# A retention layer with routed experts: dense 64-column state, half of the key decays on ScalarE, ranks from the one-hots, and routing put ahead of two weight splits

## The chip, the cores and the metric

One core of one Trainium2 chip runs the program. The metric is device microseconds (us) of one execution. TensorE is called PE here (PEld are its weight loads), VectorE DVE, ScalarE ACT, GpSimd POOL; SP issues most of the transfers (SPq is its queue).

## The reference

Three layers follow one another. With lam a decay per head (8 heads of 64, 2 batches of 768 tokens):

```python
# 1. retention, block by block (here blocks of 64; the kernel takes 128)
intra = (q_b @ k_b.T * Dmask) @ v_b
inter = (q_b * lam_pow) @ kv_state
out_b = intra + inter
kv_state = lam_block * kv_state + (k_b * rev_pow).T @ v_b
# 2. top-1 mixture of 8 experts (512 -> 1024 -> 512) over the 1536 tokens
logits = x @ w_gate + modality_bias[modality_id]
e = argmax(logits); gate = softmax(logits)[e]
y = gate * (relu(x @ w1[e]) @ w2[e])
# 3. dense layer (512 -> 2048 -> 512)
h = y @ w_in
out = (h * clip(h + 3, 0, 6) / 6) @ w_out
```

## The kernel before

Every engine but POOL runs its instructions in the order in which the program writes them, so a wait holds up whatever is written behind it on that engine. There are three stages.

**Retention** runs over 12 units `u`: 6 chunks `c` of 128 tokens, batch `b` 0 and 1 in turn. On PE a unit is: `scores(u+1)` (q against k, 64 rows by 64 rows, two PSUM banks), `rows(u-1)` (the finished unit turned to token rows and multiplied with the gate weights, tiles `xr`), `cross(u)` (q times state, `o_ps`, and decayed keys times v, `s_ps`), `inner(u)` (masked scores times v, also into `o_ps`). The state of two heads is a 128x128 block with zeros off the diagonal, so one full-array product serves both heads. POOL computes the decays (`k_d`, `q_d`, the decayed state `s_new`), DVE the masks `s_t`, the two `add`s of `s_ps` into `s_new`, and the routing; ACT copies `o_ps` to `x_t` and `xr` to `x_r` and multiplies `x_r` by the gate.

**Routing** is done once for each pair of units: `choose` (argmax as a one-hot `oh_all`), `rank` (how many earlier tokens chose the same expert: a triangle product plus a running count `acc_oh`), `place` (gate and place), `spot` (place as two one-hots, from which `sort_tokens` later writes the token lists to `order_d`).

**Experts** take slots of 264 tokens. The first, `LEAD`, is filled from the first four chunks while the last chunk is still being routed. A slot has eight pieces of weights: four of `w1` (`step` computes two hidden blocks `h_hi`, `h_lo` each) and four of `w2` (one output block each). `w_split(n)` cuts a weight into two parts: ACT writes the high one (`whi`), DVE, or POOL for pieces 0 and 1, the low one (`wlo`). `step` calls `w_split(n+2)` first. After each block `pump` writes a few instructions of the routing (`tail`, then `table`) into the queues; the table gives expert and tokens of the next slot, which SP reads to load weights and the token list `ix`, and POOL gathers the tokens `xg`. Then come dense blocks, in which nothing is touched.

Of the kernel before, what the change touches and what calls it, by code (L numbers as in the profile page):

```python
# [54 lines left out]
def retention_moe_ffn(ctx, tc, qT, kT, kn, vn, lam, mod, w_gate, bias, w1, w2, win, wout, out):  # L55
# [147 lines left out]
    def w_split(n, low=None):  # L203
        if n >= len(pieces):
            return
        raw = raws.pop(n)
        hi = wh.tile([P, 8, P], F32R, tag="whi", name="whi")
        lo = wh.tile([P, 8, P], F32R, tag="wlo", name="wlo")
        nc.scalar.copy(hi.rearrange("p a f -> p (a f)"), raw)  # L209
        (low or nc.vector).tensor_tensor(  # L210
            out=lo.rearrange("p a f -> p (a f)"), in0=raw,
            in1=hi.bitcast(F32).rearrange("p a f -> p (a f)"), op=ALU.subtract)
        ws[n] = (hi, lo)
# [29 lines left out]
    def step(n, fill=(), rate=4):  # L243
# [4 lines left out]
        if early:  # L248
            w_split(n + 2)
# [4 lines left out]
        if nxt is not None and s == LEAD and q == NP1 + 1:  # L254
            x_gather_next(nxt)
# [51 lines left out]
    with ExitStack() as ac:  # L307
# [66 lines left out]
        acc_oh = acon.tile([P, B, E], BF16, name="acc_oh")  # L374
        nc.gpsimd.iota(acc_oh, pattern=[[0, B], [NT // P, E]], base=0, channel_multiplier=0,
# [72 lines left out]
        def decays(u):  # L448
            b, c = units[u]
            q_t, k_t, k_n, v_n = data[u]  # L450
            if c < NC - 1:
                kdec[u] = a2.tile([P, H, D], F32, tag="k_d", name="k_d")
                nc.gpsimd.tensor_tensor(
                    out=kdec[u], in0=k_n, in1=dmask[:, :, C - 1:C].broadcast_to([P, H, D]), op=ALU.mult)
            if c > 0:
                qd[u] = a2.tile([P, NPAIR, C], F32, tag="q_d", name="q_d")
                nc.gpsimd.tensor_tensor(out=qd[u], in0=q_t, in1=qdec, op=ALU.mult)
            if c < NC - 1:
                snew[u] = a2.tile([P, NPAIR, P], F32, tag=f"st{b}", name="s_new")
                if c == 0:  # L460
                    nc.gpsimd.memset(snew[u], 0.0)
                else:
                    nc.gpsimd.tensor_tensor(
                        out=snew[u], in0=state[b], in1=qdec[:, :, C - 1:C].broadcast_to([P, NPAIR, P]), op=ALU.mult)

        def cross(u):
# [4 lines left out]
            else:  # L471
                o_ps = ps_1.tile([P, NPAIR, C], F32, tag="y0", name="o_ps")
            if c > 0:
                for p in range(NPAIR):
                    nc.tensor.matmul(o_ps[:, p, :], state[b][:, p, :], qd[u][:, p, :], start=(p == 0), stop=False)
            adds = []
            if c < NC - 1:
                s_ps = ps_1.tile([P, NPAIR, P], F32, tag="y1", name="s_ps")
                kd2 = kdec[u].rearrange("p (a t) d -> p a (t d)", t=2)
# [31 lines left out]
        def rows(u):  # L511
# [10 lines left out]
            lp = a2.tile([P, 2, E], F32, tag="lp", name="lp")  # L522
            x_r = a2.tile([P, KD, P], F32, tag="x_r", name="x_r", bufs=4)
# [7 lines left out]
        def choose(c, b0, b1, fill):  # L531

            fill = list(fill)
            n = b1 - b0
            bb = slice(b0, b1)

            def gap():
                if fill:
                    fill.pop(0)()
# [15 lines left out]
            gap()  # L555
            first = a2.tile([P, n], F32, tag="first", name="first")
            nc.vector.tensor_reduce(out=first, in_=cand, axis=AX.X, op=ALU.max)
            gap()
            nc.vector.tensor_tensor(out=oh_all[:, c, bb, :], in0=rev2, in1=e2(first), op=ALU.is_equal)
            while fill:  # L560
                gap()
# [4 lines left out]
        def rank(c, b0, b1, count=None):  # L566

            n = b1 - b0
            rk = ps_r.tile([P, n + 1, E], F32, tag="rk", name="rk")
            oh = oh_all[:, c, b0:b1, :]  # L570
            nc.tensor.matmul(rk[:, :n, :], tri_bf, oh, start=True, stop=False)
            nc.tensor.matmul(rk[:, :n, :], ones_bf, acc_oh[:, :n, :], start=False, stop=(n == 1))
            if n == 2:
                nc.tensor.matmul(rk[:, 1, :], ones_bf, oh[:, 0, :], start=False, stop=True)
            if count is not None:
                nc.tensor.matmul(rk[:, n, :], ones_bf, acc_oh[:, 0, :], start=True, stop=False)
                for j in range(n):
                    nc.tensor.matmul(rk[:, n, :], ones_bf, oh[:, j, :], start=False, stop=(j == n - 1))
# [4 lines left out]
        def scale(c, b):  # L583
            x_r = pair[c]["x"][b]
            nc.scalar.activation(x_r, x_r, ACTF.Copy, scale=pair[c]["gate", b])

        def store(c, b):
            i = c * B + b
            x_r = pair[c]["x"][b].rearrange("p k d -> p (k d)")
            nc.sync.dma_start(out=x_d[i * P:(i + 1) * P, :], in_=x_r)  # L590

        def place(c, b0, b1, late=False):
# [14 lines left out]
            if late:  # L607
                return
            add = oh[:, 0, :]
            if n == 2:  # L610
                add = a2.tile([P, E], BF16, tag="t2", name="t2")
                nc.vector.tensor_tensor(out=add, in0=oh[:, 0, :], in1=oh[:, 1, :], op=ALU.add)
            nc.vector.tensor_tensor(
                out=acc_oh, in0=acc_oh, in1=add.unsqueeze(1).broadcast_to([P, B, E]), op=ALU.add)
# [83 lines left out]
        decays(0)  # L698
        put_off = []
        for u in range(NU):  # L700
# [25 lines left out]
            o_ps, adds = cross(u)  # L726
            if done:
                choose(*done, adds)
            else:
                for a in adds:  # L730
                    a()
            if u == NU - 2:
                w_split(0, nc.gpsimd)
            inner(u, o_ps)
            if done:
# [14 lines left out]

        tail = [
            lambda: None,
            lambda: None,
            lambda: (rank(NC - 1, 0, B, n_e), place(NC - 1, 0, B, True), scale(NC - 1, 0), scale(NC - 1, 1)),
            lambda: spot(NC - 1),
        ]
        rows(NU - 1)
        choose(NC - 1, 0, B, [])
# [278 lines left out]
```

## Time and profile before

| | us |
|---|---|
| runs shown: median of 3 | 516.55 (515.56 to 517.21) |
| profiled execution, its own time | 521.23 |
| profiled execution, span from first to last instruction | 519.4 |
| PE busy in the span | 488.5 (94%) |
| DVE busy | 331.9 (64%) |
| ACT busy | 209.3 (40%) |
| POOL busy | 77.6 (15%) |

The shares are means over the three stages. Retention ends at about 81 us of the span, the lead slot at about 115 us, and the dense layer starts at about 244 us. A row of a timeline has start, duration, engine, line, operation, output <- inputs, shapes, count, and in brackets the idle time before it with what ended it.

### The profile page before, as it was taken

To read this page: it belongs to the slowest core of one execution; us is meant where nothing else is said; L and a number is where in the kernel's file an instruction comes from. 1 tells how busy PE (TensorE), PEld (TensorE's weight loads), DVE (VectorE), ACT (ScalarE), POOL (GpSimd) and SP (SyncE) were. 2 spreads that over 40 slices of the span, in tenths; PEclk is the share of its full clock that TensorE was granted. 3 is DMA by queue.
4 is the path that set the end of the run, shared out by engine and by line. 5 is a ranking of instruction groups with operands and counts; after the bars stand their busy time and mean duration, and the time that the engine had idled before them with its cause. 6 is when DMAs were issued, how large, how long until landed. Compare 5 with 4: busy or idle time off the path is not lost.

```text
span 519.4 us, 8309 instructions
## 1 busy us (share of the span) xinstructions
PE 488.5 (94%) x3136; PEld 429.7 (83%) x3136; DVE 331.9 (64%) x659; ACT 209.3 (40%) x365; POOL 77.6 (15%) x92
## 2 busy tenths in 40 slices
PE   5999888869999999996999999999999999999995
PEld 5888777859999999996888888888888888888885
DVE  4799998856769877771465463667646666523252
ACT  0233445425566655651354544433424343222230
POOL 4766351060020310000000000000000000003023
PEclk9899999988999999998899999999999999999998
DMA  4976364465686878541221220312202220002022
GB/s 142 370 241 204 120 202 149 167 205 163 215 273 203 257 209 263 201 133 25 99 84 43 80 82 3 114 47 81 79 3 84 76 85 1 1 1 81 1 81 81
DMA packets 25324, 64.25 MB, mean 124 GB/s; under 512 B 5954, under 2 KB 6053, under 8 KB 25277
## 3 DMA queue, kind: packets, MB, share of 16 engines
q1 hardware_dynamic: 22173, 57.25, 33.8%
q0 software_dynamic: 2416, 6.39, 3.9%
q8 instruction: 26, 0.43, 0.4%
q14 instruction: 21, 0.17, 0.1%
q10 hardware_dynamic: 688, 0.01, 0.1%
HBM read 57.29 MB, written 6.34 MB: 123 GB/s over the span
## 4 chain that ended last, share of the span: by engine, by line
PE 51%; POOL 0%; POOLq 0%; DVE 0%; issue 0%
PE ph L920 26%; PE po L939 25%; POOLq L1033 0%; POOL out_y L986 0%; POOL out_y L948 0%; DVE acc L946 0%; DVE row L973 0%
## 5 line engine op out<-in xcount | busy, mean ns | idle before, releaser
L925 DVE SCALAR_TENSOR_TENSOR g<-r,ph 128x512 f32<-128x512 f32 x48 | 33.0, 688 | 67.8 <-ACT r L923 67.8
L939 PE MATMUL po<-wo_hi,g_lo 128*128 128x512 f32 x188 | 74.1, 394 | 0.0
L939 PE MATMUL po<-wo_lo,g_hi 128*128 128x512 f32 x188 | 74.0, 394 | 0.0
L939 PE MATMUL po<-wo_hi,g_hi 128*128 128x512 f32 x188 | 73.1, 389 | 0.0
L210 DVE TENSOR_TENSOR wlo<-wraw,whi 128x1024 fp32r<-128x1024 f32 x46 | 56.2, 1222 | 18.1 <-ACT whi L209 18.0
L923 ACT ACTIVATE r<-ph,half 128x512 f32<-128x512 f32 x48 | 33.0, 688 | 81.0 <-PE ph L920 71.9
L920 PE MATMUL ph<-y_hi,wi_hi 128*128 128x512 f32 x192 | 53.3, 400 | 4.0 <-DVEq L881 4.0
L948 POOL DMA_INDIRECT out_y<-acc,row x11 | 10.7, 969 | 307.2 <-DVE acc L946 304.2
L929 DVE TENSOR_TENSOR g_lo<-g,g_hi 128x512 fp32r<-128x512 f32 x48 | 33.2, 693 | 33.0 <-ACT g_hi L927 33.0
L920 PE MATMUL ph<-y_lo,wi_hi 128*128 128x512 f32 x192 | 53.9, 403 | 0.0
L920 PE MATMUL ph<-y_hi,wi_lo 128*128 128x512 f32 x192 | 53.2, 399 | 0.0
L209 ACT CAST whi<-wraw 128x1024 fp32r<-128x1024 f32 x48 | 50.2, 1045 | 4.1 <-DMA wraw<-in_w 4.1
L920 PEld LDWEIGHTS ph<-y_hi,wi_hi 128*128 128x128 f32 x192 | 36.8, 192 | 12.3 <-ACTq L881 4.2
L927 ACT CAST g_hi<-g 128x512 fp32r<-128x512 f32 x48 | 29.8, 621 | 36.2 <-DVE g L925 36.2
L920 PEld LDWEIGHTS ph<-y_hi,wi_lo 128*128 128x128 f32 x192 | 36.9, 192 | 8.8
L920 PEld LDWEIGHTS ph<-y_lo,wi_hi 128*128 128x128 f32 x192 | 36.6, 191 | 8.9
L939 PEld LDWEIGHTS po<-wo_lo,g_hi 128*128 128x128 f32 x188 | 35.3, 188 | 8.6
L939 PEld LDWEIGHTS po<-wo_hi,g_hi 128*128 128x128 f32 x188 | 35.4, 188 | 8.4
L939 PEld LDWEIGHTS po<-wo_hi,g_lo 128*128 128x128 f32 x188 | 35.3, 188 | 7.4
L222 POOL DMA_INDIRECT xg<-x_d,ix x18 | 22.5, 1250 | 96.0 <-DMA ix<-order_d 65.9
L269 PE MATMUL ps<-x_hi,whi 128*128 128x264 f32 x192 | 32.2, 291 | 1.8 <-DVE h_lo L273 1.6
L269 PE MATMUL ps<-x_lo,whi 128*128 128x264 f32 x192 | 31.7, 288 | 0.0
(176 smaller groups left out, 820.4 us busy)
## 6 DMA issues: line engine op xcount, KB each, us to landing
wraw<-in_w SPq DMA_DIRECT2D x48, 512.0 KB, 3.5
raw<-in_win SPq DMA_DIRECT2D x16, 512.0 KB, 3.8
raw<-in_wout SPq DMA_DIRECT2D x16, 512.0 KB, 4.2
q_t<-in_qT SPq DMA_DIRECT2D x12, 256.0 KB, 3.5
k_t<-in_kT SPq DMA_DIRECT2D x12, 256.0 KB, 4.8
v_n<-in_vn SPq DMA_DIRECT2D x12, 256.0 KB, 4.2
x_d<-x_r SPq DMA_DIRECT2D x12, 256.0 KB, 2.0
k_n<-in_kn SPq DMA_DIRECT2D x10, 256.0 KB, 7.8
```

Source lines behind the costliest of these rows:

```text
L209: nc.scalar.copy(hi.rearrange("p a f -> p (a f)"), raw)
L210: (low or nc.vector).tensor_tensor(out=lo.rearrange("p a f -> p (a f)"), in0=raw, in1=hi.bitcast(F32).rearrange("p a f -> p (a f)"), op=AL ...
L222: ld = nc.gpsimd.indirect_dma_start(out=xg, out_offset=None, in_=x_d[0:EARLY * B * P, :] if s == LEAD else x_d[:], in_offset=bass.Indirect ...
L269: nc.tensor.matmul(ps, w[:, 4 * f2 + k, :], x[:, k, :], start=(m == 0), stop=(m == 3 * KD - 1))
L920: nc.tensor.matmul(ph, w[:, f, k, :], y[:, k, cols], start=(n == 0), stop=(n == 3 * KD - 1))
L923: nc.scalar.activation(r6, ph, ACTF.Relu, scale=1.0 / 6.0, bias=half)
L925: nc.vector.scalar_tensor_tensor(out=g, in0=r6, scalar=1.0, in1=ph, op0=ALU.min, op1=ALU.mult)
L927: nc.scalar.copy(g_hi, g)
L929: nc.vector.tensor_tensor(out=g_lo, in0=g, in1=g_hi.bitcast(F32), op=ALU.subtract)
L939: nc.tensor.matmul(pos_[t], g[:, ts], w[:, f, :], start=(f == 0 and n == 0), stop=(f == FB - 1 and n == 2))
L948: rows_apart(nc.gpsimd.indirect_dma_start(out=out, out_offset=bass.IndirectOffsetOnAxis(ap=row[:, i:i + 1], axis=0), in_=acc[:, i, :], in_ ...
```

## The change

- `s_new` has 64 columns for each pair instead of 128: no zero halves, no memset. `cross` computes each head by itself: `o_ps` from 64 rows to 64 columns (rows and columns of one half each), `s_ps` from 128 rows to 64 columns with 64 moving columns. The two `add`s become one, which runs ahead of `choose` instead of between its instructions.
- Of `k_d`, heads 0 to 3 are written by four ACT instructions (`key_decays(u+1)`, behind `inner(u)`), heads 4 to 7 by POOL. `q_d` is written in two POOL instructions, the POOL weight splits in four.
- `rows` copies all of `xr` with ACT and DVE sums the logits from the copy, instead of two sums from PSUM ahead of the copies.
- `rank` adds up the one-hots of all earlier chunks on PE, `acc_oh` is gone; gated rows go to a tile of their own, `x_s`.
- In steps 0 and 1 `w_split(n+2)` comes after the blocks; `rank` and `place` of the last pair are put behind the first step's second block (before: the second step's first), `spot` behind the second step's first. The next slot's gather is put one step earlier.

```diff
@@ w_split
+        parts = 4 if low else 1
+        for j in range(parts):
+            js = slice(j * 8 // parts, (j + 1) * 8 // parts)
+            (low or nc.vector).tensor_tensor(
+                out=lo[:, js, :], in0=raw.rearrange("p (a f) -> p a f", f=P)[:, js, :],
+                in1=hi.bitcast(F32)[:, js, :], op=ALU.subtract)
@@ step
-        if early:
+        if early and n > 1:
             w_split(n + 2)
...
-        if nxt is not None and s == LEAD and q == NP1 + 1:
+        if nxt is not None and s == LEAD and q == NP1:
             x_gather_next(nxt)
...
                 pump(fill, rate)
+            if n < 2:
+                w_split(n + 2)
@@ decays
-                    out=kdec[u], in0=k_n, in1=dmask[:, :, C - 1:C].broadcast_to([P, H, D]), op=ALU.mult)
+                    out=kdec[u][:, KA:, :], in0=k_n[:, KA:, :],
+                    in1=dmask[:, KA:, C - 1:C].broadcast_to([P, H - KA, D]), op=ALU.mult)
...
+        def key_decays(u):
+            if units[u][1] < NC - 1:
+                k_n = data[u][2]
+                for h in range(KA):
+                    nc.scalar.activation(kdec[u][:, h, :], k_n[:, h, :], ACTF.Copy, scale=dmask[:, h, C - 1:C])
@@ cross
                 for p in range(NPAIR):
-                    nc.tensor.matmul(o_ps[:, p, :], state[b][:, p, :], qd[u][:, p, :], start=(p == 0), stop=False)
+                    for r in halves:
+                        nc.tensor.matmul(
+                            o_ps[r, p, :], state[b][r, p, :], qd[u][r, p, :], start=(p == 0), stop=False)
...
-                    nc.tensor.matmul(s_ps[:, p, :], kd2[:, p, :], v_n[:, p * P:(p + 1) * P], start=True, stop=True)
+                    for t, r in enumerate(halves):
+                        h = 2 * p + t
+                        nc.tensor.matmul(
+                            s_ps[r, p, :], kdec[u][:, h, :], v_n[:, h * D:(h + 1) * D], start=True, stop=True)
@@ rows
             for j in range(2):
-                nc.vector.tensor_reduce(
-                    out=lp[:, j, :], in_=xr[j][:, :, P:].rearrange("p k e -> p e k"), axis=AX.X, op=ALU.add)
-                nc.scalar.copy(x_r[:, 2 * j:2 * j + 2, :], xr[j][:, :, :P])
-            nc.vector.tensor_tensor(out=lg[:, b, :], in0=lp[:, 0, :], in1=lp[:, 1, :], op=ALU.add)
+                nc.scalar.copy(x_r[:, 2 * j:2 * j + 2, :], xr[j])
+            nc.vector.tensor_reduce(
+                out=lg[:, b, :], in_=x_r[:, :, P:].rearrange("p k e -> p e k"), axis=AX.X, op=ALU.add)
@@ rank
+            nc.tensor.matmul(rk, ones_bf, base_oh[:, :m, :], start=True, stop=False)
+            for a in earlier:
+                nc.tensor.matmul(rk, ones_bf, over(a, m), start=False, stop=False)
+            nc.tensor.matmul(rk[:, 1:, :], ones_bf, over(oh[:, 0, :], m - 1), start=False, stop=False)
...
+            nc.tensor.matmul(rk[:, :n, :], tri_bf, oh, start=False, stop=True)
```

How the queues change, at three places. First PE, from the ranks of chunk 1 to the end of the next unit (`rk` rank, `xr` rows, `o_ps` cross and inner, `s_ps` new state). Before:

```order
L571 LDWEIGHTS tri_bf
L571 MATMUL rk<-oh_all,tri_bf 128x16
L572 LDWEIGHTS ones_bf
L572 MATMUL rk<-acc_oh,ones_bf 128x16
L574 LDWEIGHTS ones_bf
L574 MATMUL rk<-oh_all,ones_bf 128x8
L521 MATMUL xr<-iw,x_t 128x136 x4
L475 MATMUL o_ps<-q_d,s_new 128x128 x4
L481 MATMUL s_ps<-v_n,k_d 128x128 x4
L501 MATMUL o_ps<-s_t,v_n 64x128 x8
```

And of the change, from behind the rank's first product:

```order
L583 LDWEIGHTS ones_bf
L583 MATMUL rk<-oh_all,ones_bf 128x16
L583 LDWEIGHTS ones_bf
L583 MATMUL rk<-oh_all,ones_bf 128x16
L584 LDWEIGHTS ones_bf
L584 MATMUL rk<-oh_all,ones_bf 128x8
L587 LDWEIGHTS tri_bf
L587 MATMUL rk<-oh_all,tri_bf 128x16
L539 MATMUL xr<-iw,x_t 128x136 x4
L491 MATMUL o_ps<-q_d,s_new 64x128 x8
L499 MATMUL s_ps<-v_n,k_d 64x64 x8
L519 MATMUL o_ps<-s_t,v_n 64x128 x8
```

The state's two groups have eight half-size products each instead of four, and the rank two products more for each earlier chunk.

Second ACT, from one unit's `x_t` to the next unit's `x_t`, with what each instruction waits for. Before:

```order
L505 COPY x_t<-o_ps 128x512 [waits PE_49,Activation_49]
L585 ACTIVATE x_r<-x_r,gate 128x512 [waits DVE_49,Activation_49]
L585 ACTIVATE x_r<-x_r,gate 128x512 [waits Activation_49]
L527 COPY x_r<-xr 128x256 [waits DMAHW2_49,DVE_49]
L527 COPY x_r<-xr 128x256 [waits DVE_49]
L505 COPY x_t<-o_ps 128x512 [waits PE_49]
```

And of the change:

```order
L523 COPY x_t<-o_ps 128x512 [waits PE_49,Activation_49]
L478 ACTIVATE k_d<-k_n,dmask 128x64 [waits DMAHW4_49,Activation_49,Pool_49]
L478 ACTIVATE k_d<-k_n,dmask 128x64 x3
L596 ACTIVATE x_s<-x_r,gate 128x512 [waits DMAHW2_49,DVE_49,Activation_49]
L596 ACTIVATE x_s<-x_r,gate 128x512 [waits DMAHW3_49,Activation_49]
L542 COPY x_r<-xr 128x272 [waits PE_49] x2
L523 COPY x_t<-o_ps 128x512 [waits PE_49]
```

The copies `x_r`, which stand ahead of `x_t`, waited for DVE and now wait for PE; four decays stand in between.

Third DVE, at the start of the lead slot, from the end of the last `choose` (`sm`) on; `wlo` is the low part of a weight, `n_e` to `gate` are the last pair's rank and place. Before:

```order
L563 TENSOR_REDUCE sm<-ex 128x2
L210 TENSOR_TENSOR wlo<-wraw,whi 128x1024
L273 SCALAR_TENSOR_TENSOR h_lo<-ps,h_hi 128x264 x2
L210 TENSOR_TENSOR wlo<-wraw,whi 128x1024
L273 SCALAR_TENSOR_TENSOR h_lo<-ps,h_hi 128x264
L580 TENSOR_TENSOR n_e<-rk,off_e 128x8
L596 TENSOR_TENSOR tmp<-rk,oh_all 128x16
L597 TENSOR_SCALAR sm<-sm 128x2
```

And of the change:

```order
L570 TENSOR_REDUCE sm<-ex 128x2
L277 SCALAR_TENSOR_TENSOR h_lo<-ps,h_hi 128x264 x2
L590 TENSOR_TENSOR n_e<-rk,off_e 128x8
L607 TENSOR_TENSOR tmp<-rk,oh_all 128x16
L608 TENSOR_SCALAR sm<-sm 128x2
L610 TENSOR_REDUCE dst_all<-tmp 128x2
L612 RECIPROCAL gate<-sm 128x2
L214 TENSOR_TENSOR wlo<-wraw,whi 128x1024
```

Two weight splits stood ahead of the last pair's rank; now they stand behind it.

## Rows read from the trace of the kernel before

**Rows 1.** Busy time by stretches: start:end, length, engines (instructions), PE clock granted, DMA share, GB/s.
```profile
39.00:52.00 13.00, 11.82 (x137) 10.80 (x134) 11.73 (x36) 4.04 (x10) 7.91 (x7) 1.00 0.62 204
...
91.00:104.00 13.00, 11.57 (x100) 11.22 (x99) 11.70 (x41) 6.48 (x12) 0.00 (x0) 1.00 0.49 167
104.00:117.00 13.00, 8.32 (x70) 7.78 (x70) 7.27 (x15) 3.79 (x7) 7.98 (x6) 0.87 0.68 204
```

**Rows 2.** Timeline of one pair of units: the wait, then PE's groups.
```profile
41.86 1.50 DVE L626 TENSOR_TENSOR at_b<-b_io,pos_b 128x256 f16<-128x256 int32 x1
...
44.42 0.24 DVE L525 TENSOR_REDUCE lp<-xr 128x8 f32<-128x16 f32 x2
...
45.15 0.60 ACT L505 COPY x_t<-o_ps 128x512 f32<-128x512 f32 x1
...
45.80 1.19 PE L521 MATMUL xr<-iw,x_t 128*128 128x136 f32 x8 [1.18 <-ACT x_t L505]
46.72 0.98 PEld L475 LDWEIGHTS o_ps<-q_d,s_new 128*128 128x128 f32 x8
...
47.62 0.97 PEld L481 LDWEIGHTS s_ps<-v_n,k_d 128*128 128x128 f32 x8
...
48.71 0.85 PEld L501 LDWEIGHTS o_ps<-s_t,v_n 128*64 128x64 f32 x16
...
49.74 0.97 PEld L443 LDWEIGHTS sc<-q_t,k_t 64*128 64x128 f32 x16 [0.17 <-issue]
```

**Rows 3.** Waits by pair, 13 to 81 us: total us, times, longest.
```profile
PE xr L521 <- ACT x_t L505: 4.0, 4, 1.2
...
PE rk L571 <- DVE oh_all L559: 2.3, 2, 1.7
...
PE xr L521 <- ACT x_r L527: 0.5, 1, 0.5
```

**Rows 4.** Groups by line and shape, 0 to 120 us: busy us, mean ns | idle before.
```profile
L457 POOL TENSOR_TENSOR q_d<-q_t,qdec 128x512 f32<-128x512 f32 x10 | 13.1, 1306 | 16.8 <-PE o_ps L475 10.3 <-issue 4.7 <-DMA q_t<-in_qT 1.4
...
L527 ACT COPY x_r<-xr 128x256 f32<-128x256 f32 x24 | 7.8, 377 | 23.6 <-DVE lp L525 23.6
...
L489 DVE TENSOR_TENSOR s_new<-s_new,s_ps 64x256 f32<-64x256 f32 x16 | 6.6, 415 | 0.2
...
L554 DVE SCALAR_TENSOR_TENSOR cand<-df,rev_e 128x16 f32<-128x16 f32 x6 | 5.3, 878 | 0.2
...
L552 ACT ACTIVATE ex<-df 128x16 f32<-128x16 f32 x6 | 1.3, 216 | 4.0 <-DVE df L550 4.0
```

**Rows 5.** Timeline, first and last of the three products of one rank.
```profile
50.83 0.18 PE L571 MATMUL rk<-oh_all,tri_bf 128*128 128x16 bf16 x1
...
50.90 0.17 PE L574 MATMUL rk<-oh_all,ones_bf 128*128 128x8 bf16 x1
```

**Rows 6.** Timeline of the start: ACT's table load, the first state product.
```profile
2.67 1.28 ACT L505 ACT_TABLE_LOAD   x1 [2.67 <-issue]
...
13.85 2.07 PE L481 MATMUL s_ps<-v_n,k_d 128*128 128x128 f32 x8
```

**Rows 7.** Timeline of the lead slot, 82 to 115 us.
```profile
82.08 2.40 POOL L210 TENSOR_TENSOR wlo<-wraw,whi 128x1024 fp32r<-128x1024 f32 x1 [4.16 <-ACT whi L209]
82.17 2.35 DVE L546 TENSOR_TENSOR lg<-lg,bias_tok 128x16 f32<-128x16 f32 x1
...
91.69 0.43 DVE L273 SCALAR_TENSOR_TENSOR h_lo<-ps,h_hi 128x264 fp32r<-128x264 f32 x1 [1.74 <-ACT h_hi L272]
...
99.87 0.17 DVE L817 SCALAR_TENSOR_TENSOR tab<-s_io,picks 128x13 int32<-128x13 f32 x1
...
100.44 0.40 PE L290 MATMUL py<-h_lo,whi 128*128 128x264 f32 x1 [1.13 <-DVE h_lo L273]
...
101.10 0.37 SPq L219 DMA_DIRECT2D ix<-order_d  x1
...
114.66 0.85 PE L236 MATMUL xt<-ident,xg 88*128 88x88 f32 x4 [2.14 <-DMA xg<-x_d,ix]
```

More of the change, by code (lines that the diff above doesn't have):

```diff
@@ L25 @@
 B, H, S, D = 2, 8, 768, 64
+KA = 4
 NPAIR = H // 2
@@ L373, in retention_moe_ffn @@
         nc.gpsimd.memset(zrow, 0.0)
-        acc_oh = acon.tile([P, B, E], BF16, name="acc_oh")
-        nc.gpsimd.iota(acc_oh, pattern=[[0, B], [NT // P, E]], base=0, channel_multiplier=0,
+        base_oh = acon.tile([P, B + 1, E], BF16, name="base_oh")
+        nc.gpsimd.iota(base_oh, pattern=[[0, B + 1], [NT // P, E]], base=0, channel_multiplier=0,
                        allow_small_or_imprecise_dtypes=True)
@@ L568, in rank @@
             n = b1 - b0
-            rk = ps_r.tile([P, n + 1, E], F32, tag="rk", name="rk")
+            m = n + (count is not None)
+            rk = ps_r.tile([P, m, E], F32, tag="rk", name="rk")
             oh = oh_all[:, c, b0:b1, :]
[L571 to L574, printed above, removed]
+            earlier = [oh_all[:, c2, b2, :] for c2 in range(c) for b2 in range(B)]
+            over = lambda a, k: a.unsqueeze(1).broadcast_to([P, k, E])
+            nc.tensor.matmul(rk, ones_bf, base_oh[:, :m, :], start=True, stop=False)
+            for a in earlier:
+                nc.tensor.matmul(rk, ones_bf, over(a, m), start=False, stop=False)
+            nc.tensor.matmul(rk[:, 1:, :], ones_bf, over(oh[:, 0, :], m - 1), start=False, stop=False)
             if count is not None:
-                nc.tensor.matmul(rk[:, n, :], ones_bf, acc_oh[:, 0, :], start=True, stop=False)
-                for j in range(n):
-                    nc.tensor.matmul(rk[:, n, :], ones_bf, oh[:, j, :], start=False, stop=(j == n - 1))
+                nc.tensor.matmul(rk[:, n, :], ones_bf, oh[:, 1, :], start=False, stop=False)
+            nc.tensor.matmul(rk[:, :n, :], tri_bf, oh, start=False, stop=True)
+            if count is not None:
                 nc.vector.tensor_tensor(out=count, in0=rk[:, n, :], in1=off_e, op=ALU.subtract)
@@ L584, in scale @@
             x_r = pair[c]["x"][b]
-            nc.scalar.activation(x_r, x_r, ACTF.Copy, scale=pair[c]["gate", b])
+            x_s = pair[c]["s", b] = a2.tile([P, KD, P], F32, tag="x_s", name="x_s")
+            nc.scalar.activation(x_s, x_r[:, :, :P], ACTF.Copy, scale=pair[c]["gate", b])
         def store(c, b):
             i = c * B + b
-            x_r = pair[c]["x"][b].rearrange("p k d -> p (k d)")
-            nc.sync.dma_start(out=x_d[i * P:(i + 1) * P, :], in_=x_r)
+            x_s = pair[c]["s", b].rearrange("p k d -> p (k d)")
+            nc.sync.dma_start(out=x_d[i * P:(i + 1) * P, :], in_=x_s)
         def place(c, b0, b1, late=False):
@@ L606, in place @@
                     store(c, b)
[L607 to L614, printed above, removed]
         def spot(c):
@@ L698, in retention_moe_ffn @@
         decays(0)
+        key_decays(0)
         put_off = []
@@ L726, in retention_moe_ffn @@
             o_ps, adds = cross(u)
+            for a in adds:
+                a()
             if done:
[L728 to L731, printed above, removed]
+                choose(*done)
             if u == NU - 2:
@@ L734, in retention_moe_ffn @@
             inner(u, o_ps)
+            if u + 1 < NU:
+                key_decays(u + 1)
             if done:
@@ L749, in retention_moe_ffn @@
                 lead_order()
+        rows(NU - 1)
+        choose(NC - 1, 0, B)
         tail = [
             lambda: None,
+            lambda: (rank(NC - 1, 0, B, n_e), place(NC - 1, 0, B, True)),
+            lambda: (spot(NC - 1), scale(NC - 1, 0), scale(NC - 1, 1)),
             lambda: None,
-            lambda: (rank(NC - 1, 0, B, n_e), place(NC - 1, 0, B, True), scale(NC - 1, 0), scale(NC - 1, 1)),
-            lambda: spot(NC - 1),
-        ]
-        rows(NU - 1)
-        choose(NC - 1, 0, B, [])
+        ]
         step(0, tail, 1)
```

41 lines of the change are left out of this document (14 added, 27 removed).

## The prediction

> **What bounds the kernel now.** I read the busy time by stretches first. From 39 to 52 us PE is busy 11.82 of 13 us and DVE 11.73, so neither covers for the other; in the lead slot (91 to 104) DVE has 11.70 and PE 11.57; from 104 to 117 PE has only 8.32 and its granted clock falls to 0.87, between the two levels [rows 1]. Behind that the dense layer keeps PE busy and nothing of it is changed, so what the change is worth is how much earlier PE gets through the first 117 us.
>
> Where PE waits in retention the waits by pair say: 4.0 us for `x_t` (four times), 2.3 us for a one-hot (twice), 0.5 us for `x_r` [rows 3]. The timeline shows the cause of the first: DVE's `at_b` takes 1.50 us, so the logit sums `lp` start only at 44.42; the `x_r` copies wait for them, `x_t` stands behind those in ACT's queue and starts at 45.15, and PE has waited 1.18 us when `xr` starts at 45.80 [rows 2]. It is late DVE work seen through ACT. In the lead slot a DVE addition of 16 elements runs from 82.17 to 84.52, as long as POOL's weight split, 82.08 to 84.48 [rows 7]. From there DVE is late to the end: PE waits 1.13 us for `h_lo` at 100.44, the table entry `tab` that names the next slot's tokens is started at 99.87, SP asks for the list at 101.10, and the last gathered tokens reach PE at 114.66 after 2.14 us of waiting [rows 7]. Those steps are a chain, so what is earlier at `tab` is earlier at 114.66.
>
> **The change part by part** (a minus is a gain).
>
> *ACT no longer waits for DVE.* `x_r` waits for PE alone, so the waits for `x_t` and `x_r` should go: -4.0 and -0.5 [rows 3]. ACT takes on four decays a unit. No row shows one; a 16-element activation takes 0.216 and a 256-element copy 0.377 [rows 4], so four cost 0.9 to 1.5 us. I take 1.0, as 64 elements lie near the small one. They stand behind `x_t` and are needed one scores, one rows and one cross group later: 1.03 (16 records, as in `inner`, 48.71 to 49.74) + 0.92 (45.80 to 46.72) + 0.90 (46.72 to 47.62) = 2.85 us [rows 2], so they are hidden; behind them wait the gate products and `x_r`, with ACT at 4.04 of 13 us [rows 1]. If that cover were gone, up to 1.5 us a unit would be on the path. At the start the table load (1.28 us, at 2.67 before, hidden) now stands with the first decay behind the keys' transfer; POOL's decay released the first state product at 13.85 [rows 6]. Bounds 0 and +1.3; I take 0, because PE then needs only half of the heads from ACT first and one at a time.
>
> *PE, cross.* Four full products take 0.90 us (46.72 to 47.62), 0.11 us for each of 8 records; the 16 records of `inner`, on two column halves, take 1.03 us and so 0.064 each, because the halves overlap [rows 2]. The 16 new records of `o_ps` work on two quarters. Nearest are the other half-array groups at 0.064: 1.03 us, and about 0.1 for one more change of the array's form (`s_ps`, 8 records, takes 1.09 where `o_ps` takes 0.90, and is followed by such a change [rows 2]). That is +0.22 a unit, 10 units: +2.2. `s_ps` has 16 records with half the moving columns: at most 1.03, at least about half, 0.55; I take 0.85, between, nearer to the row, for 1.09: -0.24 a unit, 10 units, -2.4 (bounds -0.6 and -5.4). Together -0.2.
>
> The timeline shows no group in which two row halves write into one PSUM bank: `scores` gives each half its own, and `inner` has column halves. The Trainium skill's "TensorEngine Tiling (Array Packing)" (Restrictions and Gotchas) says that different row tiles cannot access the same bank at once, and the new `o_ps` does that, on different partitions. By the row the group costs 1.03 us, by the rule it would be one quarter after another; that is the first rival.
>
> *Ranks.* 26 more products over the five pairs behind the first (2, 4, 4, 8, 8). Two steps of one rank are 0.07 us apart, 0.035 each [rows 5]: +0.9. Below it could be nothing, where PE waits for the one-hot anyway.
>
> *DVE.* `add` is one instruction instead of two (-0.415 a unit [rows 4]); `acc_oh` goes; the logit sum is one instruction. `choose` now stands behind an `add` that needs `s_ps`, so it ends later against PE: I take +0.2 for each of three pairs and +0.3 at the pair before the lead is chosen, +0.9 (bounds 0 and +4). The rank wait of 1.7 us [rows 3] ends a stretch in which DVE alone is behind (ranks, lead places, masks, `choose`): one `add`, one logit sum and the running count less give -0.9 there. POOL's instructions are shorter (`q_d` 1306 ns, `cand` on DVE 878 on average for 16 elements [rows 4]); where DVE waits for POOL it is for pieces of half the length. In steady units that is now hidden behind PE, so I count nothing.
>
> Retention: -4.0 - 0.5 - 0.2 + 0.9 + 0.9 - 0.9 = -3.8.
>
> *Lead slot.* The addition's 2.35 us were almost all waiting. With four POOL pieces DVE waits for one, 2.40 / 4 = 0.6 [rows 7]: -2.2 + 0.6. The logit sum has to wait for two copies at 0.377 [rows 4], of which about 0.3 shows: +0.3. At 91.69 DVE idles 1.74 us for `h_hi`, which is behind the gate products on ACT [rows 7]; with rank and place earlier I expect 0.7: -1.0. The two splits that moved cost DVE the same, only later, and their blocks are needed two steps on; the four ranks, places and one-hots that pass them come earlier by that much. Sum at `tab`: -2.3. The gather is asked for as soon as `tab` is there; in SP's queue it now passes one weight load (piece 8), which then runs beside the gather. I count no cost; bounds 0 and +1.5.
>
> The rule that fits the 2.35 us is in the Trainium skill's "SBUF — State Buffer" (Who interferes with whom): two SBUF inputs on DVE and a GpSimd read share a port, and the second to issue waits for the whole instruction. The ends at 84.48 and 84.52 agree. Whether DVE gets in between pieces that follow closely no row shows: third rival.
>
> **Sum.** -3.8 - 2.3 = -6.1. The profiled execution's 521.23 us would be 515.1; it stands 4.7 above the median of the runs, 516.55, from which I forecast 510.4.
>
> **Rivals.**
> 1. *The quarters take turns* (slower). Then each of the 16 records of `o_ps` needs 0.11 us, as a full one does [rows 2]: 1.78 for 1.03, +0.75 a unit, +7.5: -6.1 + 7.5 = +1.4, 518.0. It decides from 0.064 + 6.1/160 = 0.102 us a record. For it: scores keep separate banks. Against: `inner` overlaps in one bank.
> 2. *`choose` becomes the wait.* If POOL's pieces hit its first and middle instructions, PE waits 1.0 more at three ranks: 513.4. For it: `cand` at 878 ns [rows 4]; against: DVE loses more work than `choose` is moved.
> 3. *The lead slot gains nothing.* DVE waits for all four pieces, or the gather lands no earlier because weights run beside it: 512.7.
> 4. *More than forecast.* `s_ps` at 0.55 us (-3.0), no later `choose` (-0.9), and half of the wait before 114.66 gone with its low clock (-1.0): 505.5.
>
> **How the numbers follow.** Forecast 0.45, rivals in order 0.13, 0.15, 0.12, 0.15. A measurement can tell about 0.3% from no change, 1.55 us. All but the first rival lie more than that below; of it about 0.08 is slower and 0.05 within; unforeseen waits (a colder clock at the start, ACT's longer queue) take another 0.03 to slower and 0.02 to within. Faster 0.82, within 0.07, slower 0.11. The range goes from 504.5 (rival 4 and a little of its clock) to 515.5 (rivals 2 and 3 together, 510.4 + 3.0 + 2.3 = 515.7, nearly); rival 1 is left out.
>
> **What would show it.** Right: no PE wait on `x_t`; pairs of units about 1.2 us shorter; `o_ps` groups of 16 in 1.0 to 1.1 us; the first addition of the last `choose` at 0.8 us or less; `tab` about 15 us behind that addition (82.17 to 99.87 before, 17.7) and the last gather earlier with it. Wrong: `o_ps` groups near 1.8 us, waits of `rk` on `oh_all` at each pair, or a state product waiting for ACT's decays.

## The result, and the profile after

The changed kernel takes 509.38 us (median of 4 runs, 508.42 to 509.76) where the kernel before takes 516.41 (4 runs, 515.56 to 517.21): a ratio of 0.9861, 95% interval 0.984 to 0.9883, or 7.0 us less. The profiled execution after is one of the four, 509.76 us with a span of 507.8.

Busy time by stretches, the changed kernel, columns as in [rows 1]:

```profile
39.00:52.00 13.00, 12.58 (x207) 10.97 (x205) 8.83 (x33) 8.28 (x23) 7.25 (x11) 1.00 0.66 212
...
91.00:104.00 13.00, 8.99 (x81) 8.62 (x81) 9.85 (x25) 4.58 (x7) 4.91 (x3) 1.00 0.82 236
104.00:117.00 13.00, 12.85 (x95) 12.77 (x96) 8.24 (x13) 7.47 (x14) 2.96 (x3) 0.87 0.56 167
```

Against [rows 1], DVE has 8.83 us in a stretch of retention for 11.73, and ACT 8.28 for 4.04. DVE is no longer nearly full there, though PE still waits for it at the ranks (below). The stretches are not the same work in the lead slot, since everything is some 7 to 10 us earlier: what stood in 104 to 117 before, PE at 8.32 and waiting, now stands in 91 to 104, PE at 8.99.

Timeline of PE, the changed kernel, one unit, the rank of the next, and the end of the pair:

```profile
31.02 1.16 PE L449 MATMUL sc<-q_t,k_t 64*128 64x128 f32 x16
32.11 1.19 PE L539 MATMUL xr<-iw,x_t 128*128 128x136 f32 x8
33.24 1.09 PE L491 MATMUL o_ps<-q_d,s_new 64*64 64x128 f32 x16
34.26 0.69 PE L499 MATMUL s_ps<-v_n,k_d 128*64 128x64 f32 x16
34.77 1.05 PE L519 MATMUL o_ps<-s_t,v_n 128*64 128x128 f32 x16
35.75 1.16 PE L449 MATMUL sc<-q_t,k_t 64*128 64x128 f32 x16
...
37.51 0.17 PE L584 MATMUL rk<-oh_all,ones_bf 128*128 128x8 bf16 x1 [0.44 <-DVE oh_all L568]
...
41.17 1.16 PE L449 MATMUL sc<-q_t,k_t 64*128 64x128 f32 x16
```

The shown durations overlap, so a group is read from its start to the next one's. The 16 records of `o_ps` on quarters take 1.02 us, those of `s_ps` 0.51. From the scores of unit 4 (31.02) to those of unit 6 (41.17) it is 10.15 us; before it was 11.37. `xr` starts without a wait. The waits by pair, 13 to 78 us, answer to [rows 3]:

```profile
PE rk L584 <- DVE oh_all L568: 2.9, 5, 0.9
PE s_ps L499 <- ACT k_d L478: 0.2, 1, 0.2
```

The 4.0 and 0.5 us for `x_t` and `x_r` are gone; the wait for the one-hot is 2.9 us in five places, where it was 2.3 in two (in a second profile of the kernel before, run 1, 2.9 in three). Two signs that the prediction named as wrong are there too: a rank wait at each pair, and a state product that waits for ACT's decays, once, 0.2 us. Timeline of the lead slot, the changed kernel, for [rows 7]:

```profile
73.97 0.73 PE L273 MATMUL ps<-x_hi,whi 128*128 128x264 f32 x4
...
74.87 2.82 POOL L214 TENSOR_TENSOR wlo<-wraw,whi 128x256 fp32r<-128x256 f32 x4 [2.21 <-ACT whi L210]
...
75.65 0.69 DVE L557 TENSOR_TENSOR lg<-lg,bias_tok 128x16 f32<-128x16 f32 x1
...
76.58 0.46 DVE L561 TENSOR_TENSOR df<-lg,mx 128x16 f32<-128x16 f32 x1
77.07 0.66 DVE L565 SCALAR_TENSOR_TENSOR cand<-df,rev_e 128x16 f32<-128x16 f32 x1
...
77.96 0.17 DVE L568 TENSOR_TENSOR oh_all<-rev_e,first 128x16 bf16<-128x16 f32 x1
...
90.78 0.17 DVE L822 SCALAR_TENSOR_TENSOR tab<-s_io,picks 128x13 int32<-128x13 f32 x1
91.73 0.37 SPq L223 DMA_DIRECT2D ix<-order_d  x1
...
94.45 1.03 POOL L226 DMA_INDIRECT xg<-x_d,ix  x1 [16.75 <-DMA ix<-order_d]
...
97.36 1.75 DVE L863 TENSOR_TENSOR at_b<-b_io,pos_b 128x1536 f16<-128x1536 int32 x1
97.63 2.34 POOL L226 DMA_INDIRECT xg<-x_d,ix  x1 [0.30 <-issue]
...
104.15 0.96 PE L240 MATMUL xt<-ident,xg 88*128 88x88 f32 x8 [2.17 <-DMA xg<-x_d,ix]
```

The same choice in the kernel before ends here:

```profile
85.37 0.17 DVE L559 TENSOR_TENSOR oh_all<-rev_e,first 128x16 bf16<-128x16 f32 x1
```

The addition takes 0.69 us for 2.35, but `df` and `cand` take 0.46 and 0.66 behind it where small instructions of the same choice take 0.17: with four pieces of about 0.7 us from 74.87 on, each of the three ends within 0.1 us of the end of a piece, so DVE waits for three of the four, one after another. From the addition's start to the end of the one-hot it is 2.48 us for 3.37. The table entry comes 15.1 us behind the addition's start for 17.7, and PE again waits 2.17 us for the second and third group of gathered tokens.

The profile before stood 4.7 us above the median of its runs, so a difference of the two traces overstates the gain. The first run below settles where the 4.7 us sit.

### The profile page after: what moved, and what is told of

Its sections match the earlier page's. It is cut to its first block, busy times and chain, and to the rows that moved or that the text cites. A ratio compares the mean times of both kernels' runs of the same rounds, so it can differ in the third digit from the quotient of the medians.

```text
span 507.8 us, 8695 instructions
## 1 busy us (share of the span) xinstructions
PE 483.7 (95%) x3322; PEld 424.1 (84%) x3322; DVE 315.1 (62%) x615; ACT 219.5 (43%) x405; POOL 71.6 (14%) x106
## 4 chain that ended last, share of the span: by engine, by line
PE 53%; POOL 0%; POOLq 0%; DVE 0%; issue 0%
PE ph L925 27%; PE po L944 26%; POOLq L1038 0%; POOL out_y L991 0%; POOL out_y L953 0%; DVE acc L951 0%; DVE row L978 0%
## 5 line engine op out<-in xcount | busy, mean ns | idle before, releaser
L925 PEld LDWEIGHTS ph<-y_hi,wi_hi 128*128 128x128 f32 x192 | 36.9, 193 | 12.4 <-ACTq L886 4.2
L932 ACT CAST g_hi<-g 128x512 fp32r<-128x512 f32 x48 | 29.8, 621 | 36.2 <-DVE g L930 36.2
```

The source lines that it names most:

```text
L925: nc.tensor.matmul(ph, w[:, f, k, :], y[:, k, cols], start=(n == 0), stop=(n == 3 * KD - 1))
L932: nc.scalar.copy(g_hi, g)
```

## The experiments

Each run also lists the kernel before on the same chip. There it scattered more than in the runs above: 513.5 to 520.6 us around 516.75 (17 runs, first four experiments), 515.1 to 522.4 around 517.62 (23, next four), 515.3 to 520.8 around 519.10 (11, last four). So times are compared as ratios or within a chip, and single terms are read from the traces, between two marks: from PE's scores of unit 4 to the first block of the lead slot (its first `ps` product). There the granted clock is 1.00, but for some 4 us in the profiles of runs 7 and 8, where it falls to 0.57; and there two profiles of one kernel agree within 0.02 us. All in us:

| kernel | from unit 4's scores to the lead slot | units 4 and 5 |
|---|---|---|
| before; its second profile | 49.03; 49.02 | 11.37; 11.35 |
| before + rows part alone | 47.59 (4 us at a low clock) | 10.95 |
| before + dense state alone | 46.06 (4 us at a low clock) | 11.11 |
| changed; its second profile | 42.95; 42.97 | 10.15; 10.16 |
| changed, rows part undone | 44.22 | 10.15 |
| changed, dense state undone | 45.66 | 11.04 |
| changed, GpSimd and ScalarE part undone | 43.54 | 10.50 |
| changed, lead part undone | 42.94 | 10.15 |
| changed, addition behind the choice | 40.78 | 9.57 |

**1. Before, again.** No edit.

> The kernel before, unchanged, profiled a second time. Its first profile stands 4.7 us above the median of its runs. If that excess is a matter of the one execution, this profile comes out at 516 to 517 us, and the place where its rows are earlier than in the first one is where the 4.7 us sat; my guess is the stretch behind the gather wait (104 to 130 us), where the granted clock fell. If it belongs to profiled executions of this kernel, it is again near 521 us.

It took 516.46 us. Timeline, the kernel before, second profile:

```profile
81.04 0.75 PE L269 MATMUL ps<-x_hi,whi 128*128 128x264 f32 x4 [0.15 <-ACT x_hi L238]
...
99.82 0.17 DVE L817 SCALAR_TENSOR_TENSOR tab<-s_io,picks 128x13 int32<-128x13 f32 x1
...
112.07 1.07 PE L236 MATMUL xt<-ident,xg 88*128 88x88 f32 x12
```

The table entry is where it was (99.82 for 99.87), but all twelve transposes run at 112.07 with no wait, where the first profile's last ones stood at 114.66; the granted clock from 117 to 130 is 1.00 for 0.87. The dense layer starts at 239.87 for 244.41. So the 4.7 us lie between the table and the dense layer: the gather's landing, and the clock behind it, as guessed. Against this profile the change brings 7.1 us at the lead slot (81.04 to 73.97), 9.0 at the table, 7.9 at the last transposes (112.07 to 104.15), 7.3 at the dense layer (239.87 to 232.61) and 6.9 in the span.

**2. Rows part undone.**

```diff
-            x_r = a2.tile([P, KD, W], F32, tag="x_r", name="x_r", bufs=4)
+            x_r = a2.tile([P, KD, P], F32, tag="x_r", name="x_r", bufs=4)
             for j in range(2):
-                nc.scalar.copy(x_r[:, 2 * j:2 * j + 2, :], xr[j])
-            nc.vector.tensor_reduce(out=lg[:, b, :], in_=x_r[:, :, P:]...)
+                nc.vector.tensor_reduce(out=lp[:, j, :], in_=xr[j][:, :, P:]...)
+                nc.scalar.copy(x_r[:, 2 * j:2 * j + 2, :], xr[j][:, :, :P])
```

> The changed kernel, but with the logit sums taken from PSUM ahead of the x_r copies again, so that ACT waits for DVE. Theory A (my prediction: this wait is worth 4.0 for x_t and 0.5 for x_r, less 0.3 in the lead slot): 509.4 + 4.2 = about 513.6 us, with PE waits on x_t of some 1 us in three or four pairs. Rival B (DVE has lost so much other work, additions, running counts, locked time, that its sums come in time anyway): 509.4 to 510.4 us, and no PE wait on x_t of over 0.3 us.

509.09 us, ratio 0.9834 (0.9778 to 0.989): rival B, but for one `x_t` wait of 0.49 us, above the 0.3 it allowed. Timeline of the same place as [rows 2], this kernel:

```profile
40.79 0.42 DVE L631 TENSOR_TENSOR at_b<-b_io,pos_b 128x256 f16<-128x256 int32 x1
...
41.40 0.25 DVE L543 TENSOR_REDUCE lp<-xr 128x8 f32<-128x16 f32 x2
...
42.55 0.58 ACT L523 COPY x_t<-o_ps 128x512 f32<-128x512 f32 x1 [0.26 <-PE o_ps L519]
...
43.52 1.19 PE L539 MATMUL xr<-iw,x_t 128*128 128x136 f32 x8
```

`at_b` takes 0.42 us here for the 1.50 of [rows 2], the sums `lp` start 1.15 us ahead of `x_t` for 0.73, and ACT is free when `o_ps` is done: it waits 0.26 for PE, not for DVE. The pair is 10.15 us with or without this part. Only the last two units lose by it: of 1.27 us up to the lead slot, 0.49 is the one `x_t` wait that is left.

**3. Dense state undone** (`cross`, `s_new` and the two additions as before, in the changed kernel).

```diff
-                    for r in halves:
-                        nc.tensor.matmul(o_ps[r, p, :], state[b][r, p, :], qd[u][r, p, :], ...)
+                    nc.tensor.matmul(o_ps[:, p, :], state[b][:, p, :], qd[u][:, p, :], ...)
...
-                adds = [add]
+                adds = [lambda: add(0), lambda: add(1)]
```

> The changed kernel with the state as 128 by 128 blocks with zero halves again (full cross products, two additions on DVE, 512 elements on GpSimd for the decayed state). Theory A (my prediction: the new PE groups cost 0.2 us less in all, the rest is hidden): within 1 us of 509.4. Rival B (the after trace: the state products cost 0.46 us a unit and not 0.85, so the groups save about 0.4 us in each of 10 units): about 513.4 us. Rival C (the additions and the longer GpSimd instruction show on DVE as well): 515 us or more, with waits of PE for DVE inside the pairs.

513.90 us, ratio 0.993 (0.9896 to 0.9963): rival B. Timeline of PE, one unit of this kernel and the next rank:

```profile
44.95 1.16 PE L449 MATMUL sc<-q_t,k_t 64*128 64x128 f32 x16
46.05 1.19 PE L537 MATMUL xr<-iw,x_t 128*128 128x136 f32 x8
47.08 1.05 PE L491 MATMUL o_ps<-q_d,s_new 128*128 128x128 f32 x8
47.97 1.06 PE L497 MATMUL s_ps<-v_n,k_d 128*128 128x128 f32 x8
48.95 1.09 PE L517 MATMUL o_ps<-s_t,v_n 128*64 128x128 f32 x16
49.98 1.16 PE L449 MATMUL sc<-q_t,k_t 64*128 64x128 f32 x16
...
51.97 0.17 PE L582 MATMUL rk<-oh_all,ones_bf 128*128 128x8 bf16 x1 [0.62 <-DVE oh_all L566]
```

From start to start the unit is 5.03 us; the changed kernel's, above, 4.73. `xr` and `o_ps` together cost 2.15 for 1.92 (+0.23, the change of the array's form included), `s_ps` and `inner` 1.49 for 2.01 (-0.52). A pair differs by 0.89 us: 0.60 of PE's products, and 0.18 of the rest is the longer rank wait (0.62 for 0.44). Of the 2.71 us up to the lead slot the rank waits make 1.26 (3.69 for 2.43) and PE's products nearly all the rest.

**4. Lead part undone.**

```diff
-        if early and n > 1:
+        if early:
             w_split(n + 2)
...
-        if nxt is not None and s == LEAD and q == NP1:
+        if nxt is not None and s == LEAD and q == NP1 + 1:
...
-        parts = 4 if low else 1
+        parts = 1
...
-            if n < 2:
-                w_split(n + 2)
```

(`tail` is as before too.)

> The changed kernel with the lead slot's order of before: weight splits ahead of the blocks, GpSimd's split in one piece, ranks and places two blocks later, the gather one piece later. Theory A (my prediction, 2.3 us at the table): about 511.7 us, with the first addition of the last choice near 2.3 us long. Rival B (the after trace: 2 us at the table and 1.8 us more between gather and first slot, with the clock): about 513.2 us. Rival C (another wait takes its place): within 0.5 us of 509.4.

509.23 us, ratio 0.9869 (0.9809 to 0.9928). Timeline, this kernel:

```profile
74.36 0.74 PE L273 MATMUL ps<-x_hi,whi 128*128 128x264 f32 x4
...
76.02 1.67 DVE L555 TENSOR_TENSOR lg<-lg,bias_tok 128x16 f32<-128x16 f32 x1
...
93.06 0.17 DVE L820 SCALAR_TENSOR_TENSOR tab<-s_io,picks 128x13 int32<-128x13 f32 x1
...
105.53 1.07 PE L240 MATMUL xt<-ident,xg 88*128 88x88 f32 x12
```

From first block to table it is 18.70 us, as before (18.75), and 16.81 in the changed kernel: 1.9 us, near theory A's 2.3, though the addition takes 1.67 us and not 2.3. But here the tokens are all there at 105.53, 12.5 us behind the table, while the changed kernel waits until 104.15, 13.4 behind its own. The time doesn't tell the kernels apart, as rival C has it. Three more runs look for what holds the gather.

**5. Changed, again.** No edit.

> The changed kernel itself, timed and profiled once more on the same chip as the next three: the base for them. If the wait of 2.17 us for the gathered tokens at 104.15 belongs to the kernel, it stands here again and the time is about 509.4 us; if it was an accident of one execution, the transposes of the next slot run without a wait over 0.5 us and the profile is near 507.5 us.

509.65 us (6 runs, 509.32 to 511.07), ratio 0.9831 (0.9785 to 0.9878). Timeline, the changed kernel, second profile:

```profile
96.24 1.58 POOL L226 DMA_INDIRECT xg<-x_d,ix  x1 [18.06 <-DMA ix<-order_d]
...
106.61 0.85 PE L240 MATMUL xt<-ident,xg 88*128 88x88 f32 x4 [1.10 <-DMA xg<-x_d,ix]
```

The waits for tokens are there again, 2.05 and 1.10 us, and the last transposes stand at 106.61, 15.3 us behind a table entry at 91.27. So they belong to the kernel, and the landing scatters by some 2 us. Of the scatter 1.3 us lie ahead of the gather itself, in the read of its list: SP asks for it 0.95 us behind the table in both profiles, and POOL's first issue starts 2.7 us behind that request in the first (91.73 to 94.45) and 4.0 in this one (92.21 to 96.24).

**6. Gather behind weight load 8.**

```diff
-        if nxt is not None and s == LEAD and q == NP1:
+        if nxt is not None and s == LEAD and q == NP1 + 1:
             x_gather_next(nxt)
```

> The changed kernel with one thing undone: SP asks for the gather's list one piece later again, behind weight load 8. Theory A (the gather's 512 KB neighbour in the queue delays it: gathers took a median of 6.3 us to land after the change, 4.7 us with the lead part undone): table entry still near 90.8, no wait over 0.5 us for the gathered tokens, about 507.4 us. Rival B (my prediction's zero for the passed load): the same as the changed kernel within 0.5 us. Rival C (the list now waits for load 8): table near 90.8 but the list later than 93, and the time 510 us or more.

510.80 us (506.12 to 512.62), ratio 0.9824 (0.9769 to 0.988), against 509.65 of the run before on the same chip. Theory A's gain doesn't show: the last transposes still wait 1.50 us, at 105.80, 14.3 behind the table. The list is asked for at 92.72, so of rival C only the time is met. Rival B is nearest, but the median is 1.15 us above run 5 where B allowed 0.5, in runs that scatter over 6.5 us.

**7. Rows part alone**, on the kernel before (the edit of run 2 the other way, with `x_s`).

> The kernel before with one part of the change alone: x_r copied first with its logit columns, sums taken from SBUF afterwards, so that ACT never waits for DVE. Theory A (my prediction: the waits for x_t, 4.0, and x_r, 0.5, go and nothing takes their place): 516.6 - 4.5 = about 512.1 us, a pair of units in 10.2 us. Rival B (DVE's work fills the pair, and the wait turns up at the masks or the one-hot instead): a pair stays at 11.2 to 11.4 us and the time at 515.5 to 516.6 us.

514.20 us, ratio 0.993 (0.9896 to 0.9964). The kernel before took 517.62 on this chip, so by the time the part gains 3.4 us (by the interval 1.9 to 5.4). The profiled execution is 7 us above this median, with a low clock behind 104 us; only its retention is read. Waits by pair, 13 to 78 us, then the clock (columns as in [rows 1]) and two groups of PE in it:

```profile
PE rk L569 <- DVE oh_all L557: 3.4, 4, 1.3
PE rk L569 <- issue: 1.8, 1, 1.8
```

```profile
74.00:78.00 4.00, 4.00 (x30) 3.55 (x29) 3.23 (x7) 2.25 (x5) 1.95 (x1) 0.57 0.66 227
```

```profile
74.16 1.65 PE L501 MATMUL o_ps<-s_t,v_n 128*64 128x128 f32 x16
75.73 2.18 PE L521 MATMUL xr<-iw,x_t 128*128 128x136 f32 x8
```

No wait for `x_t` is left, but between the marks the waits at the ranks are 4.6 us for 2.3. (Of the second row the trace names no releaser; it is the rank of the pair before the gather, at 73.00, and DVE's one-hot ends at 72.94.) A pair gains 0.42 us of 1.18. Up to the rank at 73.00 the part gains 1.9 us. Up to the lead slot it gains 1.44, but from 74 to 78 us the granted clock is 0.57, and the two groups above, 1.57 and 1.98 us to the next one's start where they take 1.02 and 1.03 at full clock, cost 1.5; without that it would be at most about 2.9. So it lies between A and B: the pairs are nearer to B, the time is nearer to A.

**8. Dense state alone**, on the kernel before (the edit of run 3 the other way).

> The kernel before with one part of the change alone: the dense state (16 records on quarters for the cross products, half columns for the state products, one addition for two, half the decayed state on GpSimd). Theory A (PE's groups are shorter by 0.45 us a unit, but ACT still waits for DVE's sums, so the gain goes into a longer x_t wait): a pair at 11.1 to 11.4 us and 515 to 516.6 us. Rival B (one addition less is enough for DVE's sums to come in time, and both gains show): a pair at 10.2 to 10.6 us and about 511 us.

514.10 us, ratio 0.9925 (0.9882 to 0.9968). Timeline, this kernel:

```profile
43.88 1.19 PE L523 MATMUL xr<-iw,x_t 128*128 128x136 f32 x8 [0.62 <-ACT x_t L507]
```

The `x_t` wait is halved, 0.62 for 1.18, though ACT still stands behind DVE's sums; 0.56 less is near one addition (0.415, [rows 4]). Units 6 and 7 take 10.22 us, as rival B has it; units 4 and 5 take 11.11, as theory A has it, with one wait of 1.52 for a mask. The stretch is 2.97 less, and 2.9 already at the scores of unit 10, ahead of the low clock (0.57 from 66 to 70 us). The time, 3.5 us less than the kernel before on this chip, lies between the two.

**9 and 10. at_b out of the lead slot**, in the changed kernel, and in the one with the lead part undone.

```diff
+        *[lambda: None] * 12,
         lambda: V.tensor_tensor(
             out=at_b, in0=b_io.unsqueeze(1).broadcast_to([P, NTILE, P]),
```

> The changed kernel with at_b of all twelve tiles (DVE, 1.75 us, and the row products that read it) moved out of the lead slot into the next one, so that DVE leaves GpSimd alone while it issues the three gathers. Theory A (the gather chain from table to last landing, 13 to 15 us, is what bounds the next slot, and its third issue takes 2.3 us for 1.0 because of at_b): the three issues end about 1.3 us earlier, PE's 1.63 us wait for at_b is gone too, and the time is 507.5 to 508.3 us against 509.4 to 509.7 of the changed kernel. Rival B (the transfers themselves, beside the weight loads, are the limit): the issues are shorter, but the last tokens land as late, and the time stays within 0.5 us of the changed kernel.

> The same move of at_b, in the changed kernel with the lead part undone (splits ahead of blocks, GpSimd's split in one piece, ranks two blocks later). Theory A (the lead part does bring the table 1.9 us forward, and only the gather hid it): about 1.9 us slower than the changed kernel with at_b moved, so about 509.5 us. Rival B (the next slot starts when PE has done the lead slot's products, and the table comes early enough in both): within 0.5 us of it.

510.80 us, ratio 0.9852 (0.9819 to 0.9886), and 513.75, ratio 0.9909 (0.9874 to 0.9943). Timelines, the first and then the second:

```profile
90.69 0.17 DVE L822 SCALAR_TENSOR_TENSOR tab<-s_io,picks 128x13 int32<-128x13 f32 x1
...
97.53 1.81 POOL L226 DMA_INDIRECT xg<-x_d,ix  x1 [0.30 <-issue]
...
103.90 1.29 PE L240 MATMUL xt<-ident,xg 88*128 88x88 f32 x8 [2.37 <-DMA xg<-x_d,ix]
```

```profile
93.48 0.17 DVE L820 SCALAR_TENSOR_TENSOR tab<-s_io,picks 128x13 int32<-128x13 f32 x1
...
107.84 0.85 PE L240 MATMUL xt<-ident,xg 88*128 88x88 f32 x4 [1.08 <-DMA xg<-x_d,ix]
```

In run 9 the third issue is 0.5 us shorter and PE's wait for `at_b` is gone, but a wait of 1.64 for the first tokens stands in its place, the last tokens come 13.2 us behind the table for 13.4, and the ratio is no better. That is rival B's sign; that the transfers are the limit is not shown by one profile, with a landing that scatters by some 2 us. With PE's `at_b` wait out of both, the lead part shows: 2.95 us between the two, on one chip, over theory A's 1.9. In this pair of profiles the later one also has the lower clock behind the wait (0.74 for 0.87 from 104 to 117).

**11. Addition behind the choice**, with at_b moved as in run 9.

```diff
-            for a in adds:
-                a()
             if done:
                 choose(*done)
+            for a in adds:
+                a()
```

> at_b moved as in the two runs before, and in retention the state addition put behind the choice instead of ahead of it. Theory A (my prediction's term: the choice ends later because it stands behind an addition that needs the state products; the rank waits are now 0.43 to 0.92 us in each of five pairs): rank waits fall by 0.3 to 0.45 us each, 1.5 to 2 us in all, about 506 us. Rival B (the addition is then late for the next pair's decayed state, or its work only changes places on DVE): rank waits as before, and the time within 0.5 us of at_b moved alone.

508.36 us (507.19 to 510.05), ratio 0.9804 (0.9768 to 0.9839), 2.4 less than run 9 on the same chip. Busy time from 39 to 52 us, and the last one-hot product of a rank, now without a wait, this kernel:

```profile
39.00:52.00 13.00, 13.00 (x209) 11.46 (x206) 9.37 (x31) 9.01 (x26) 8.05 (x12) 1.00 0.69 231
```

```profile
36.88 0.17 PE L584 MATMUL rk<-oh_all,ones_bf 128*128 128x8 bf16 x1
```

Theory A, and more: four of the five rank waits are gone, PE is busy without a gap, a pair takes 9.57 us and the stretch 2.2 less. It has the lowest ratio of the kernels here that keep the whole change; its interval ends just below that of the first result (0.984 to 0.9883), but overlaps that of run 5.

**12. GpSimd and ScalarE part undone.**

```diff
-KA = 4
+KA = 0
...
-                for p in range(0, NPAIR, 2):
-                    nc.gpsimd.tensor_tensor(out=qd[u][:, p:p + 2, :], ...)
+                nc.gpsimd.tensor_tensor(out=qd[u], in0=q_t, in1=qdec, op=ALU.mult)
```

> The changed kernel with all key decays on GpSimd in one instruction and the query decays in one instead of two. Theory A (my prediction: the decays on ACT are hidden and the shorter pieces gain nothing that shows): within 0.5 us of 509.5 us, first block of the lead slot as early, counted from the fourth unit's scores. Rival B (DVE now waits for GpSimd's longer pieces inside the choice, and the rank waits grow): 0.3 us more in each of five pairs and so about 511 us.

508.43 us (506.49 to 513.2), ratio 0.9801 (0.9764 to 0.9838): no loss. Its trace shows rival B's mechanism, rank waits of 0.72 to 0.81 in the early pairs for 0.42 to 0.51: 0.35 us more a pair early on, but only 0.6 up to the lead slot, where B had 0.3 in each of five pairs. Why the time is no longer, or even shorter, stays open; its one profile is of its slowest execution.

## Why the prediction was right

The forecast, 510.4 us, holds, and so does the size of the gain. In part that is luck: retention gave 2.3 us more than forecast, mainly because one group of products was mis-sized, and the lead slot passed on less of its gain than forecast.

- **x_t and x_r, -4.5.** In the whole change the waits went, as said, and between the marks nothing grew in their place: the rank waits are 2.43 us there for 2.31. What is wrong is the cause. The prediction gave the 4.5 us to one part, ACT's copies no longer waiting for DVE. Taken out of the changed kernel, that part costs only 1.3 (run 2), since the other parts relieve DVE so far that its sums come in time anyway. Alone it gains 1.9 to 2.9 (run 7), since the waits at the ranks grow from 2.3 to 4.6. DVE was the pair's second bound [rows 1], and a wait removed from the path of such an engine came back at the next place where PE asks for it. The place is that of rival 2; rival 2's cause, POOL's pieces, was not in that run.
- **Cross and state products, -0.2: the term that was mis-sized.** Cross was right: +0.22 a unit, measured +0.23. The state products were not: -0.24 a unit taken, -0.52 measured with `inner` behind them, close to the far bound (0.51 us for the group, 0.55 named as the least). Over 10 units that would be -2.9 for -0.2. Between the marks, with eight of the cross groups and six of the state groups, undoing the dense state costs 2.7, nearly half of it in rank waits (run 3). That is rival 4's first part, true.
- **Ranks +0.9, choice +0.9, DVE -0.9.** All three came out between the marks: the rank products take 1.6 us for 0.5, the long rank wait fell from 1.7 to 0.65 (-1.0), and the others rose from 0.65 to 1.8 (+1.1). Run 11 shows the cause of the last and that more was to be had: the addition that waits for PE, put behind the choice instead of ahead of it, makes the stretch 2.2 us shorter. No run undoes the ranks alone.
- **ACT's key decays, 0, and the start, 0.** No cost shows: PE waits 0.2 us for them once, at the start, and undoing them gains nothing in the trace.
- **Retention, -3.8.** Measured -6.1 from unit 4 to the lead slot, -7.1 with the start, which scatters with the clock. PE's groups, read from start to start, account for the -6.1: waits 7.0 us to 2.4, products other than the ranks' 41.5 to 38.9, the ranks' +1.1.
- **Lead slot, -2.3.** -1.9 at the table, but not piece by piece. The choice starts 0.6 us later behind the first block (taken: +0.3, for the logit sum). The addition takes one POOL piece (2.82 / 4 = 0.7), as said, but `df` and `cand` wait for a piece each, so the choice gains 0.9 and not 1.6. What stands behind it gains 1.7 for 1.0. Passing weight load 8: no cost shows (run 6), within a scatter of several us. The step "what is earlier at `tab` is earlier at 114.66" holds only on average, because the landing scatters by as much. From first block to last transposes the eight profiles with the new lead part take 29.8 to 32.2 us (mean 30.5), the six with the old one 31.0 to 33.5 (mean 32.2), counted to the start of the last group.
- **Rival 1** fell: 0.064 us a record. **Rival 3** fell for the addition, though DVE waited for three of the four pieces, at one instruction each; for the gather its second half is partly true in single executions (run 4 against the first profile after).

So retention gave 2.3 more than forecast, the lead slot 1.9 at the table and by the times anything from 0.4 (run 4 against the first result) to 3.0 (runs 9 and 10), and the medians 7.0 for 6.1. Between the second profile before and the first after, 9.0 us at the table are 7.9 at the transposes and 6.9 at the end. What sets the landing of the gathered tokens, 12.4 to 15.3 us behind the table where PE waits for it, is not settled: moving `at_b` or load 8 made no difference beyond the scatter, and a gather with no weight load near it was not tried.

## What to carry to other kernels

When two engines are both nearly full in a stretch, a wait between them doesn't belong to the part that removes it: ask of each removed wait what the late engine is asked for next, and make one variant with that part alone and one without it. Where a stretch of the trace serves as a ruler, read its granted clock in every run that is measured with it; in two runs here 4 us at a low clock lay inside the ruler, and in one of them it hid up to 1.5 us of the gain. Where an instruction needs the busiest engine's newest result, write it behind the work that engine is itself waiting for. Before a term rests on a single transfer's landing, take a second profile of the same kernel; here one execution's late gather and the low clock behind it were worth 4.7 us, over half of the whole gain.

## What the hardware showed that was not expected

- Two row halves wrote side by side into one PSUM bank, on different partitions: 16 records of `o_ps` on quarters in 1.02 us, 0.064 each, as those of `inner` on column halves, where a full record takes 0.11 [rows 2]; one after another they would have taken 1.78. The Trainium skill's "TensorEngine Tiling (Array Packing)" (Restrictions and Gotchas) says that different row tiles cannot access the same bank at once; this trace doesn't show it.
- Products of 128 rows to 64 columns with 64 moving columns took 0.51 us for 16, 0.032 each, half of the 0.064 with 128.
- A DVE addition got in between POOL's pieces: 0.69 us, one piece, where the whole instruction had held it for 2.35. Two later instructions of the choice, 0.46 and 0.66 us for 0.17, were each held up by a further piece. The Trainium skill's "SBUF — State Buffer" (Who interferes with whom) says that the second to issue waits for the whole instruction, and the trace agrees, with the piece as the instruction.
- The granted clock in the first stretch of work (13 to 26 us) was anything from 0.74 to 0.91 in the fourteen profiles, and the scores of unit 4 stood between 30.9 and 34.3 us. Part of that is the edits; in the six profiles whose retention is the changed kernel's, with a clock of 0.79 to 0.88, they stood between 30.9 and 31.8.
